# A new opening for a fused recurrence and feed-forward kernel: larger first blocks and rows, casts held back, and more inputs turned by the transposing DMA

## The chip, the cores and the metric

The kernel runs on one core of one Trainium2 chip. The metric is the device time of one execution in microseconds (us). The median of the kernel before is 418.55 us over four runs (418.23 to 419.21).

## The reference

Two stages, fused in the kernel. The first is a gated recurrence along the sequence, independent for each of 4 sequences and 256 channels; the second is a feed-forward layer with the maximum of two projections.

```python
sig = 1.0 / (1.0 + np.exp(-f_logit))                    # x, f_logit: 4 x 6144 x 256, float32
f = lower_bound + (1.0 - lower_bound) * sig             # lower_bound: 256
for t in range(S):
    h = f[:, t] * h + (1.0 - f[:, t]) * x[:, t]
    y[:, t] = h
h1, h2 = y @ w1, y @ w2                                 # w1, w2: 256 x 1024
return np.maximum(h1, h2) @ w_out                       # w_out: 1024 x 256
```

## The kernel before

The kernel walks through 24,576 tokens in blocks of 512. It runs the recurrence as scans on DVE with channels on partitions (128 x 512, 1.26 us each), so f and x have to be turned from token-major to channel-major. There are two ways to do that, chosen per chunk of 1024 tokens:

- **By PE.** GpSimd starts a DMA that casts the float32 chunk to bfloat16 in SBUF, and PE transposes it in tiles of 128 x 128.
- **By the transposing DMA.** GpSimd starts a DMA that casts the chunk into a scratch buffer in DRAM; when it has landed, SP starts a transposing DMA from there into SBUF (`fT`, `xT`). There are six scratch buffers for f and six for x.

```python
sizes = [256, 256, 512] if b == 0 else []              # first chunks of the first sequence
sizes += [CH] * ((S - sum(sizes)) // CH)               # CH = 1024
...
def by_xbar(c, s):                                     # s: 0 is f, 1 is x
    return c >= 5 and (s == 0 or c % 4 != 3)
...
NSCR = 6
scratch = [[dram.tile([CH, D], BF16, name=f"scr{s}_{q}") for q in range(NSCR)] for s in range(2)]
...
def fetch(c):
    ...
        elif by_xbar(c, s):
            scr = scratch[s][uses[s] % NSCR]
            uses[s] += 1
            nc.gpsimd.dma_start(out=scr[0:nt, :].rearrange("(p i) d -> p (i d)", p=P),
                                in_=src.rearrange("(p i) d -> p (i d)", p=P))
            held[c, s] = scr
        else:
            nat = natpool.tile([P, CH // P, D], BF16, name=("fn", "xn")[s])
            nc.gpsimd.dma_start(out=nat[:, 0 : nt // P, :],
                                in_=src.rearrange("(i p) d -> p i d", p=P))

def cross(c):
    ...
            nc.sync.dma_start_transpose(out=dst[:, :, 0:nt], in_=held[c, s][0:nt, :])
...
def gate(j):                                           # Sigmoid on ACT, from fT or from PSUM
    nc.scalar.activation(out=u[:, :, 0:nb], in_=turned[j, 0], func=AF.Sigmoid, scale=-1.0)
...
LEAD_FETCH = 10                                        # how many blocks ahead casts are written down
LEAD_CROSS = 5                                         # the same for transposing DMAs
...
for j in range(1, NBLK + 1):
    ahead("fetch", fetch, j + LEAD_FETCH)
    ahead("cross", cross, j + LEAD_CROSS)
    for fc in range(FC):                               # eight slots per block
        if j < NBLK:
            first_layer(j, fc)                         # 2 matmuls of 512 columns, Relu on ACT
        second_layer(j - 1, fc)                        # 5 matmuls of 256 columns
        ...                                            # an eighth of the PE transposes of block j + 2
        if fc < len(scans):
            scans[fc]()                                # a step of the recurrence of block j + 1, on DVE
        if fc == FC // 2 and j + 2 < NBLK:
            gate(j + 2)
```

GpSimd runs its list of casts as fast as it can. Apart from waits, mostly of about 2 us, for an earlier DMA to land, what stops it is a scratch buffer whose transpose has not been read yet. The main loop has no hold on it.

## Time and profile before

| | before |
|---|---|
| time, median | 418.55 us |
| PE busy | 395.5 of 415.8 us |
| a steady block of 512 tokens | 7.82 us, or 8.26 us with 8 PE transposes of x in it |
| main loop begins | 25.7 us |
| first transposing DMA for f: issued, landed | 33.3, 64.0 us |

The first lines are of the profile page of the kernel before: the span, PE's busy row, and three rows of 40 slices of 10.4 us each. A digit is the busy share in tenths, PEclk the granted clock in tenths.

```profile
span 415.8 us, 7247 instructions
PE 395.5 (95%) x2872; PEld 304.8 (73%) x2920; DVE 239.3 (58%) x354; ACT 274.1 (66%) x457; POOL 30.9 (7%) x57
...
PE   2699997999999999999999999999999999999996
...
PEclk9989998999999999999999999999999999999999
DMA  8998989999799999999999999872852453811212
```

PE sets the pace once it runs; what is lost is lost early, in the first two slices and in the seventh (62 to 73 us). The next lines are of the chain of waits of the kernel before (start us, duration us, what), from its early part.

```profile
2.50 6.76 DMA xn<-in_x_dram
...
9.54 23.77 DMA scr_0_90<-in_f_logit_dram
...
33.33 30.69 DMA fT<-scr_0_90
```

Up to 64 us the chain is nearly all DMA. One transposing DMA of half a megabyte takes 30.69 us, and PE then stands still for lack of it. The stretches of 5 us (busy us of each engine, granted clock, DMA share, GB/s) show how much:

```profile
55.00:60.00 5.00, 4.95 (x38) 3.72 (x35) 2.79 (x6) 2.92 (x6) 0.00 (x0) 1.00 1.01 218
60.00:65.00 5.00, 2.88 (x21) 2.14 (x20) 2.76 (x3) 0.98 (x2) 0.46 (x1) 1.00 0.86 149
65.00:70.00 5.00, 4.29 (x21) 2.59 (x21) 1.22 (x3) 3.11 (x7) 0.94 (x2) 0.66 1.10 270
```

The first number after the length is PE: 4.95, then 2.88, then 4.29 us at a clock of 0.66. The waits of 40 to 80 us (who waited for whom: us, times, longest) name both sides of it:

```profile
POOL scr_0_90 L104 <- DMA fT<-scr_0_90: 22.8, 1, 22.8
...
ACT u L160 <- DMA fT<-scr_0_90: 4.0, 1, 4.0
```

ACT wanted the data 4.0 us before they came. GpSimd (POOL) had run out of free scratch buffers 22.8 us before.

### The profile page before, as it was taken

What the parts mean: (1) busy time and instruction counts of PE and PEld (TensorE: products, weight loads), DVE (VectorE), ACT (ScalarE), POOL (GpSimd) and SP (SyncE); (2) the same over time, 40 slices, a digit from 0 to 9 for tenths busy, and PEclk for the clock granted to TensorE, in tenths of its full rate; (3) what the DMA queues carried; (4) which work ended last, traced back from release to release, by engine and by line L of the source; (5) the groups of instructions that cost most, each with busy time, mean ns of one, the idle gap of its engine ahead of it and who ended that gap; (6) DMA issues with size and microseconds to landing.
All of it is one profiled execution on the core that took longest, in us unless ns stands there. A gap on an engine that the chain in (4) does not pass through costs nothing.

```text
span 415.8 us, 7247 instructions
## 1 busy us (share of the span) xinstructions
PE 395.5 (95%) x2872; PEld 304.8 (73%) x2920; DVE 239.3 (58%) x354; ACT 274.1 (66%) x457; POOL 30.9 (7%) x57
## 2 busy tenths in 40 slices
PE   2699997999999999999999999999999999999996
PEld 2487774777777777777777777777777777777775
DVE  2545563665665764665665566566476575566641
ACT  2667655766766766776776676676676676677662
POOL 8122001000001000010010010000000000000000
PEclk9989998999999999999999999999999999999999
DMA  8998989999799999999999999872852453811212
GB/s 192 233 232 199 223 178 230 261 240 110 135 196 217 268 249 122 237 207 173 245 251 192 184 224 251 202 177 89 192 123 82 151 112 92 203 52 50 99 54 102
DMA packets 100657, 73.09 MB, mean 176 GB/s; under 512 B 79040, under 2 KB 93888, under 8 KB 100032
## 3 DMA queue, kind: packets, MB, share of 16 engines
q1 hardware_dynamic: 87152, 46.93, 49.4%
q0 software_dynamic: 13184, 25.43, 37.6%
q8 instruction: 23, 0.38, 0.3%
q10 hardware_dynamic: 288, 0.26, 0.2%
q14 instruction: 10, 0.08, 0.1%
HBM read 53.48 MB, written 44.56 MB: 236 GB/s over the span
## 4 chain that ended last, share of the span: by engine, by line
PE 83%; DMA 15%; issue 1%; ACT 0%; POOL 0%; DVE 0%; POOLq 0%; ACTq 0%
PE psO L330 48%; PE dT L301 34%; DMA fT<-scr_0_90 7%; DMA scr_0_90<-in_f_logit_dram 6%; DMA xn<-in_x_dram 2%; PE tT L151 1%; ACT u L160 0%; POOL fn L111 0%; ACT rt L309 0%; DVE osb L339 0%; POOL ident_f masks.py:199 0%; POOL ident_f masks.py:197 0%; POOLq masks.py:199 0%; ACTq L160 0%; POOLq L439 0%
## 5 line engine op out<-in xcount | busy, mean ns | idle before, releaser
L309 ACT ACTIVATE rt<-dT 128x512 bf16<-128x512 f32 (+1 forms) x392 | 225.7, 587 | 117.8 <-PE dT L301 115.7
L330 PE MATMUL psO<-wob,rt 128*128 128x256 bf16 x1536 | 230.8, 273 | 2.3
L301 PE MATMUL dT<-y,wd 128*128 128x512 bf16 (+1 forms) x736 | 221.6, 378 | 10.1 <-DVE wd L257 7.0
L330 PEld LDWEIGHTS <-rt 128*128 128x128 bf16 x1536 | 169.6, 113 | 42.9 <-issue 0.6
L350 DVE COPY osb<-psO 128x512 f32<-128x512 f32 x94 | 65.0, 692 | 153.0 <-PE psO L330 153.0
L194 DVE TENSOR_TENSOR_SCAN y<-ff,y,v 128x512 bf16<-128x512 bf16 (+1 forms) x90 | 109.2, 1255 | 0.0
L301 PEld LDWEIGHTS <-wd 128*128 128x128 bf16 x784 | 71.9, 98 | 16.9 <-DVE wd L257 9.5
L330 PE MATMUL psO<-w_122,y 128*128 128x256 bf16 x384 | 73.7, 273 | 0.3
L330 PEld LDWEIGHTS <-y 128*128 128x128 bf16 x384 | 43.3, 113 | 41.6 <-issue 0.6
L160 ACT ACTIVATE u<-fT 128x1024 bf16<-128x1024 bf16 x42 | 44.0, 1048 | 4.0 <-DMA fT<-scr_0_90 4.0
L174 DVE TENSOR_SCALAR ff<-u,nom 128x512 bf16<-128x512 bf16 (+1 forms) x98 | 29.7, 347 | 0.0
L151 PE MATMUL tT<-ident,xn 128*128 128x128 bf16 x124 | 23.6, 228 | 0.0
L184 DVE TENSOR_TENSOR v<-u,xT 128x1024 bf16<-128x1024 bf16 x32 | 21.8, 681 | 2.2 <-DMA xT<-scr_0_96 2.2
L184 DVE TENSOR_TENSOR v<-u,tT 128x1024 bf16<-128x1024 bf16 (+1 forms) x17 | 11.3, 664 | 7.6 <-PE tT L151 4.0
L151 PEld LDWEIGHTS <-xn 128*128 128x128 bf16 x124 | 12.3, 103 | 0.3
L251 ACT ACTIVATE w1s<-w1n,om 128x256 f32<-128x256 f32 x8 | 3.6, 500 | 7.1 <-DMA w1n<-in_moe_w_dram 7.1
L194 DVE TENSOR_TENSOR_SCAN y<-ff,v 128x512 bf16<-128x512 bf16 (+1 forms) x8 | 8.3, 1074 | 0.0
L111 POOL DMA_DIRECT2D xn<-in_x_dram x9 | 7.9, 883 | 2.3 <-DMA xn<-in_x_dram 2.2
L160 ACT ACTIVATE u<-tT 128x1024 bf16<-128x1024 bf16 (+2 forms) x7 | 6.3, 898 | 2.1 <-PE tT L151 2.1
L257 DVE SCALAR_TENSOR_TENSOR wd<-w2n,om,w1s 128x256 bf16<-128x256 f32 x8 | 3.5, 479 | 4.5 <-ACT w1s L251 4.5
L151 PE MATMUL tT<-ident,fn 128*128 128x128 bf16 x44 | 6.1, 245 | 0.0
L104 POOL DMA_DIRECT2D scr_0_90<-in_f_logit_dram x4 | 2.0, 500 | 49.5 <-DMA fT<-scr_0_90 49.0
(40 smaller groups left out, 49.0 us busy)
## 6 DMA issues: line engine op xcount, KB each, us to landing
out_dram<-osb SPq DMA_DIRECT2D x46, 512.0 KB, 3.8
xn<-in_x_dram POOLq DMA_DIRECT2D x7, 512.0 KB, 15.0
scr_0_90<-in_f_logit_dram POOLq DMA_DIRECT2D x4, 512.0 KB, 9.0
scr_1_91<-in_f_logit_dram POOLq DMA_DIRECT2D x4, 512.0 KB, 7.3
scr_2_92<-in_f_logit_dram POOLq DMA_DIRECT2D x4, 512.0 KB, 14.1
scr_0_96<-in_x_dram POOLq DMA_DIRECT2D x3, 512.0 KB, 19.9
scr_1_97<-in_x_dram POOLq DMA_DIRECT2D x3, 512.0 KB, 9.9
scr_3_93<-in_f_logit_dram POOLq DMA_DIRECT2D x3, 512.0 KB, 8.6
```

The source lines that it names most:

```text
L111: nc.gpsimd.dma_start(out=nat[:, 0 : nt // P, :], in_=src.rearrange("(i p) d -> p i d", p=P),)
L151: nc.tensor.transpose(dst, src, ident[:] if src.dtype == BF16 else ident_f[:])
L160: nc.scalar.activation(out=u[:, :, 0:nb], in_=turned[j, 0], func=AF.Sigmoid, scale=-1.0)
L174: nc.vector.tensor_scalar(out=ff[:, h, 0:nb], in0=u[:, h, 0:nb], scalar1=nom[:, h : h + 1], scalar2=1.0, op0=ALU.mult, op1=ALU.add,)
L184: nc.vector.tensor_tensor(out=v[:, :, 0:nb], in0=u[:, :, 0:nb], in1=turned[j, 1], op=ALU.mult)
L194: nc.vector.tensor_tensor_scan(out=y[:, h, 0:nb], data0=ff[:, h, 0:nb], data1=v[:, h, 0:nb], initial=init, op0=ALU.mult, op1=ALU.add,)
L251: nc.scalar.mul(w1s[:, kc, gcols(g)], w1n[:, kc, gcols(g)], om[:, kc : kc + 1])
L257: nc.vector.scalar_tensor_tensor(out=wd[:, kc, gcols(g)], in0=w2n[:, kc, gcols(g)], scalar=om[:, kc : kc + 1], in1=w1s[:, kc, gcols(g)], o ...
L301: nc.tensor.matmul(dT[:, 0:nb], lhsT=wd[:, kc, fc * P : (fc + 1) * P], rhs=y[:, kc, 0:nb], start=(kc == 0), stop=(kc == KC - 1),)
L309: nc.scalar.activation(out=rt[:, 0:nb], in_=dT[:, 0:nb], func=AF.Relu)
L330: nc.tensor.matmul(ps[:, r, :], lhsT=left, rhs=right, start=(s == 0 and (r == 0 or j == NBLK - 1)), stop=(s == n - 1 and (r == 1 or j == N ...
L350: nc.vector.tensor_copy(out=osb[:, 2 * g : 2 * g + 2, :], in_=ps[:])
```

## The change

Its intent is to start the main loop earlier and take work off PE. The first chunks get 512 tokens, the weights come in halves with rows of 2 KB instead of quarters with rows of 1 KB, and f and x of the first chunk in rows of 4 KB. Casts wait until the weights are nearly in, by two copies of a single column (128 x 1) on GpSimd that read the weights' tiles. In exchange f is turned by DMA from the fifth chunk on (index 4), and x from the sixth on without exception. Cut to its core:

```diff
-        sizes = [256, 256, 512] if b == 0 else []
+        sizes = [TB] * 4 if b == 0 else []
@@
     def by_xbar(c, s):
-        return c >= 5 and (s == 0 or c % 4 != 3)
+        return c >= (4, 5)[s]
@@ fetch, first chunk: a plain load in 4 KB rows, then a cast on DVE
-                    out=nat[:], in_=src.rearrange("(i p) d -> p i d", p=P)
-                )
+                    out=raw[:], in_=src.rearrange("(p i) d -> p i d", p=P)
+                )
+                nat = natpool.tile([P, CH // P, D], BF16, name=("fn", "xn")[s])
+                nc.vector.tensor_copy(out=nat[:, 0 : nt // P, :], in_=raw[:])
@@ fetch, other chunks for PE: four neighbouring tokens in one row
-                    in_=src.rearrange("(i p) d -> p i d", p=P),
+                    in_=src.rearrange("(k p i) d -> p k (i d)", p=P, i=TB // P),
@@ weights
-    NG = 4
+    NG = 2
+    def pool_waits(t):
+        nc.gpsimd.tensor_copy(out=waited[:], in_=t)
@@
-    LEAD_CROSS = 5
+    LEAD_CROSS = 3
@@ opening
+        pool_waits(w1n[0][:, 0, 0:1])
+        nc.gpsimd.dma_start(out=wob[:]..., in_=moe_w_out...)
+        pool_waits(w2n[1][:, 0, 0:1])
+        ...                                        # first layer of block 0 here
+        fetch(1)
+        fetch(2)
+        ...
-        for j in range(1, NBLK + 1):
+        for j in range(2, NBLK + 1):
@@ loop: the Sigmoid of a block turned by DMA now stands in slot 0 of the block before it
+            if j + 1 < NBLK and by_xbar(blocks[j + 1][3], 0):
+                gates[0] = j + 1
```

(Left out: the PE transposes write, and ACT and DVE read, in an order that suits the new rows; the opening runs blocks 0 and 1 outside the loop.)

More of the change, by code (lines that the diff above doesn't have):

```diff
@@ L95, in fetch @@
             if c == 0:
-                nat = const.tile([P, nt // P, D], FP32, name=("f0", "x0")[s])
+                raw = const.tile([P, nt // P, D], FP32, name=("f0", "x0")[s])
                 nc.sync.dma_start(
-                    out=nat[:], in_=src.rearrange("(i p) d -> p i d", p=P)
+                    out=raw[:], in_=src.rearrange("(p i) d -> p i d", p=P)
                 )
+                nat = natpool.tile([P, CH // P, D], BF16, name=("fn", "xn")[s])
+                nc.vector.tensor_copy(out=nat[:, 0 : nt // P, :], in_=raw[:])
                 held[c, s] = nat
@@ L111, in fetch @@
                 nc.gpsimd.dma_start(
-                    out=nat[:, 0 : nt // P, :],
-                    in_=src.rearrange("(i p) d -> p i d", p=P),
+                    out=nat[:, 0 : nt // P, :].rearrange(
+                        "p (k i) d -> p k (i d)", i=TB // P
+                    ),
+                    in_=src.rearrange(
+                        "(k p i) d -> p k (i d)", p=P, i=TB // P
+                    ),
                 )
@@ L133, in turn_steps @@
                 continue
-            if c == 0:
-                dst = ps_t.tile([P, KC, nb], FP32, name="tT")
-            else:
-                dst = ps_t.tile([P, KC, TB], BF16, name="tT")
-            turned[j, s] = dst[:, :, 0:nb]
-            for q in range(nb // P):
+            dst = ps_t.tile([P, KC, TB], BF16, name="tT")
+            ns = nb // P
+            turned[j, s] = dst[:, :, 0:nb].rearrange("p k (i m) -> p k m i", i=ns)
+            for q in range(ns):
                 for h in range(KC):
@@ L150, in turn @@
         for dst, src in steps:
-            nc.tensor.transpose(dst, src, ident[:] if src.dtype == BF16 else ident_f[:])
+            nc.tensor.transpose(dst, src, ident[:])
     ys = {}
@@ L159, in gate, with like @@
         u = midpool.tile([P, KC, TB], BF16, name="u")
+        src = turned[j, 0]
         nc.scalar.activation(
-            out=u[:, :, 0:nb], in_=turned[j, 0], func=AF.Sigmoid, scale=-1.0
+            out=like(u[:, :, 0:nb], src), in_=src, func=AF.Sigmoid, scale=-1.0
         )
         us[j] = u
+    def like(t, src):
+        if len(src.shape) == 3:
+            return t
+        return t.rearrange("p k (m i) -> p k m i", m=P)
     def scan_steps(j):
@@ L183, in drive @@
         def drive():
+            src = turned[j, 1]
             nc.vector.tensor_tensor(
-                out=v[:, :, 0:nb], in0=u[:, :, 0:nb], in1=turned[j, 1], op=ALU.mult
+                out=like(v[:, :, 0:nb], src),
+                in0=like(u[:, :, 0:nb], src),
+                in1=src,
+                op=ALU.mult,
             )
@@ L218 @@
     ident = const.tile([P, P], BF16)
-    nc.vector.tensor_copy(out=ident[:], in_=ident_f[:])
     om = const.tile([P, KC], FP32)
@@ L222 @@
     lbc = const.tile([P, KC], FP32)
+    waited = const.tile([P, 1], FP32)
     warm = const.tile([P, 1], FP32)
-    nc.sync.dma_start(out=lbc[:], in_=lower_bound.rearrange("(h p) -> p h", p=P))
-    nc.vector.tensor_scalar(
-        out=om[:], in0=lbc[:], scalar1=-1.0, scalar2=1.0, op0=ALU.mult, op1=ALU.add
-    )
-    nc.vector.tensor_scalar_add(out=nom[:], in0=lbc[:], scalar1=-1.0)
-    w1n = wpool.tile([P, KC, DFF], FP32)
-    w2n = wpool.tile([P, KC, DFF], FP32)
     wob = wpool.tile([P, FC, D], BF16)
@@ L236, with half, fcs @@
     w13 = wpool.tile([P, KC, D], BF16)
-    NG = 4
-    def gcols(g):
-        return slice(g * DFF // NG, (g + 1) * DFF // NG)
+    NG = 2
+    NQ = FC // NG
+    w1n = [wpool.tile([P, KC, NQ * P], FP32, name=f"w1n{g}") for g in range(NG)]
+    w2n = [wpool.tile([P, KC, NQ * P], FP32, name=f"w2n{g}") for g in range(NG)]
+    def half(w, g):
+        return w[g][:].rearrange("p kc (m q) -> p kc q m", q=NQ)
+    def fcs(w, kc, g):
+        return w[:, kc, g * NQ * P : (g + 1) * NQ * P].rearrange(
+            "p (q m) -> p q m", q=NQ
+        )
     def fetch_w(g):
+        cols = slice(g * DFF // NG, (g + 1) * DFF // NG)
         for w, src in ((w2n, moe_w2), (w1n, moe_w1)):
             nc.sync.dma_start(
-                out=w[:, :, gcols(g)],
-                in_=src[:, gcols(g)].rearrange("(kc p) f -> p kc f", p=P),
+                out=w[g][:],
+                in_=src[:, cols].rearrange("(kc p) f -> p kc f", p=P),
             )
@@ L250, in make_w1s @@
         for kc in range(KC):
-            nc.scalar.mul(
-                w1s[:, kc, gcols(g)], w1n[:, kc, gcols(g)], om[:, kc : kc + 1]
-            )
+            nc.scalar.mul(fcs(w1s, kc, g), half(w1n, g)[:, kc], om[:, kc : kc + 1])
+    def pool_waits(t):
+        nc.gpsimd.tensor_copy(out=waited[:], in_=t)
     def make_wd(g):
@@ L257, in make_wd @@
             nc.vector.scalar_tensor_tensor(
-                out=wd[:, kc, gcols(g)],
-                in0=w2n[:, kc, gcols(g)],
+                out=fcs(wd, kc, g),
+                in0=half(w2n, g)[:, kc],
                 scalar=om[:, kc : kc + 1],
-                in1=w1s[:, kc, gcols(g)],
+                in1=fcs(w1s, kc, g),
                 op0=ALU.mult,
@@ L264, in make_wd, with make_w1T @@
             )
-    def make_w1T(g):
-        n = FC // NG
-        pt = ps_o.tile([P, KC, n, P], FP32, name="psO")
+    def make_w1T(k):
+        pt = ps_o.tile([P, KC, 2, P], FP32, name="psO")
         for kc in range(KC):
-            for q in range(n):
-                fc = n * g + q
+            for q in range(2):
+                fc = 2 * k + q
                 nc.tensor.transpose(
@@ L274, in make_w1T @@
                 )
-        dst = w1T[:, n * g : n * g + n, :].rearrange("p q (k d) -> p k q d", k=KC)
-        if g % 2:
-            nc.scalar.copy(out=dst, in_=pt[:])
-        else:
-            nc.vector.tensor_copy(out=dst, in_=pt[:])
+        dst = w1T[:, 2 * k : 2 * k + 2, :].rearrange("p q (k d) -> p k q d", k=KC)
+        nc.scalar.copy(out=dst, in_=pt[:])
     def make_w13():
@@ L367 @@
     with tc.manual_schedule():
+        nc.sync.dma_start(out=lbc[:], in_=lower_bound.rearrange("(h p) -> p h", p=P))
+        nc.vector.tensor_copy(out=ident[:], in_=ident_f[:])
+        nc.vector.tensor_scalar(
+            out=om[:], in0=lbc[:], scalar1=-1.0, scalar2=1.0, op0=ALU.mult, op1=ALU.add
+        )
+        nc.vector.tensor_scalar_add(out=nom[:], in0=lbc[:], scalar1=-1.0)
         fetch(0)
-        fetch(1)
         for g in range(NG):
             fetch_w(g)
-        nc.gpsimd.dma_start(
-            out=wob[:], in_=moe_w_out.rearrange("(fc p) c -> p fc c", p=P)
-        )
-        fetch(2)
         nc.scalar.activation(out=warm[:], in_=om[:, 0:1], func=AF.Sigmoid)
@@ L383 @@
         make_w1s(1)
-        make_wd(0)
-        first_layer(0, 0)
-        first_layer(0, 1)
-        turn(turn_steps(1))
-        make_wd(1)
-        recurrence(1)
-        first_layer(0, 2)
-        first_layer(0, 3)
-        make_w1s(2)
-        make_wd(2)
+        pool_waits(w1n[0][:, 0, 0:1])
+        nc.gpsimd.dma_start(
+            out=wob[:].rearrange("p (g q) c -> p g (q c)", g=NG),
+            in_=moe_w_out.rearrange("(g p q) c -> p g (q c)", g=NG, q=NQ),
+        )
+        pool_waits(w2n[1][:, 0, 0:1])
+        make_wd(0)
+        for fc in range(0, NQ):
+            first_layer(0, fc)
+        fetch(1)
+        fetch(2)
+        done["fetch"] = 3
+        ahead("fetch", fetch, LEAD_FETCH)
+        make_wd(1)
         make_w1T(0)
         make_w1T(1)
-        first_layer(0, 4)
-        first_layer(0, 5)
-        make_w1s(3)
-        make_wd(3)
+        for fc in range(NQ, FC):
+            first_layer(0, fc)
         make_w1T(2)
-        first_layer(0, 6)
-        first_layer(0, 7)
         make_w1T(3)
-        turn(turn_steps(2))
-        gate(2)
-        make_w13()
-        done["fetch"] = 3
-        ahead("fetch", fetch, LEAD_FETCH)
-        ahead("cross", cross, LEAD_CROSS)
-        for j in range(1, NBLK + 1):
+        make_w13()
+        turn(turn_steps(1))
+        recurrence(1)
+        for fc in range(FC):
+            second_layer(0, fc)
+        turn(turn_steps(2))
+        recurrence(2)
+        for fc in range(FC):
+            first_layer(1, fc)
+        turn(turn_steps(3))
+        gate(3)
+        for j in range(2, NBLK + 1):
             ahead("fetch", fetch, j + LEAD_FETCH)
@@ L413 @@
             steps = turn_steps(j + 2) if j + 2 < NBLK else []
-            scans = scan_steps(j + 1) if j + 1 < NBLK else []
+            gates = {}
+            if j + 1 < NBLK and by_xbar(blocks[j + 1][3], 0):
+                gates[0] = j + 1
+            if j + 2 < NBLK and not by_xbar(blocks[j + 2][3], 0):
+                gates[FC // 2] = j + 2
+            scans = []
             for fc in range(FC):
@@ L420 @@
                 turn(steps[fc * n // FC : (fc + 1) * n // FC])
+                if fc in gates:
+                    gate(gates[fc])
+                if fc == 0 and j + 1 < NBLK:
+                    scans = scan_steps(j + 1)
                 if fc < len(scans):
                     scans[fc]()
-                if fc == FC // 2 and j + 2 < NBLK:
-                    gate(j + 2)
 _INS = ['x', 'f_logit', 'lower_bound', 'moe_w1', 'moe_w2', 'moe_w_out']
```

## The prediction

> **What bounds it now.** The busy table has the tensor engine (PE) at 395.5 of 415.8 us. In the timeline its stream is gapless: a slot is two 512-column matmuls (0.43 us) and five 256-column ones (0.53), a 512-token block takes 7.8 us, a PE transpose adds 0.055. The losses are early: the main loop starts at 25.7 us, PE is busy only 2.88 us of the stretch 60 to 65, and the clock halves for 3.4 us near 21 and 65 us, costing about 1.7 us each time.
>
> The chain of waits is DMA until 64.1 us: casts, then one transposing DMA (first f chunk, issued 33.3, landed 64.0). The transfer records show why: casts into DRAM move as 32 KB packets of 2.43 us, transposes as 256-byte packets of 0.018. Between 50 and 60 us each DMA engine passed about two small packets per large one, so the transpose, 128 small packets per engine, hardly moved until GpSimd ran out of scratch slots (last cast issued 41.3, drained near 61). [...]
>
> **What the change does.**
> 1. PE transposes fall from 48 f and 128 x to 32 and 48: 96 x 0.055 = 5.3 us, 4.4 of it inside the saturated loop.
> 2. Opening: 3 MiB of f, x and weights in 2 and 4 KB rows (84 and 159 ns a packet) without casts beside them land near 11 us instead of 19. Two 128x1024 casts on DVE (about 1 us each) and 512-token scans (2.45) move the first matmul from 11 to about 14 us, but eight full slots follow. The loop at j=2 starts near 31 us; against equal work 4 to 5 us earlier than before.
> 3. But casts start near 10 us, and block 4 needs the first transposed f at about 40 us, where before block 7 needed it at 61. Only the six scratch slots stop the casts of chunks 4 to 9. Chunk 4 starts near 20 us; twelve casts of 2.45 us and two outputs drain near 52; the transpose lands near 54 to 56. So I expect a PE stall of 12 to 16 us between 41 and 56 us, in block 3.
> 4. Afterwards cast, transposes and output of a chunk take about 12.5 us of DMA in 15.6 of PE: no lasting stall.
>
> **Sum.** PE resumes at 56.5; left are half a block (3.9), 44 blocks of 7.82 (344), half clock (1.7), chunk 4's x (0.5) and the end (4.7): 354.8. Span 411, time (2.5 above span) **413.5 us, range 403 to 419**. Chances: faster by over 2% 0.28, within 2% 0.67, slower 0.05.
>
> **What would show it.** Right: weights landed by 12 us; in the chain of waits the first fT DMA lasting 25 us or more, landing at 52 to 58, with the Sigmoid waiting 10 us or more for it; low PE slices at 41 to 56; 7.8 us a block throughout; 80 transposes. Wrong: fT landing before 45, or new waits for fT or xT later, since transposes are issued three blocks ahead instead of five.
>
> **What would make it wrong.** If transposes get more turns between casts, no stall: about 400 us. If casts start later or run slower, the stall grows one for one: 417 or more. A second stall at chunk 5 would add up to 3 us.

The resumption at 56.5 us and the 354.8 us after it make the span of 411.3 us.

## The result and the profile after

| | before | after | predicted |
|---|---|---|---|
| time, median | 418.55 us | 419.52 us (418.53 to 419.99) | 413.5, range 403 to 419 |
| last part of w1 reaches ACT | 19.4 us | 13.3 us | landed near 11 |
| first matmul of the first layer | 11.1 us | 13.1 us | 14 |
| first fT landed | 64.0 us | 58.6 us | 54 to 56 |
| PE's stall for it | 2.8 us | 12.8 us | 12 to 16 |
| PE resumes | 65.7 us | 60.3 us | 56.5 |
| steady blocks | 7.82 and 8.26 us | 7.82 us | 7.82 |

The ratio is 1.0018, 95% interval 0.9994 to 1.0042: the same. A ratio here is the mean time of one kernel's fast runs over that of the kernel before in the same rounds, so it is not quite the ratio of the medians quoted. The span of the profiled run was 418.2 us, its time 419.99.

The page of the kernel after, the same rows:

```profile
span 418.2 us, 6999 instructions
PE 388.8 (93%) x2761; PEld 296.7 (71%) x2808; DVE 246.5 (59%) x345; ACT 273.3 (65%) x446; POOL 27.9 (7%) x59
...
PE   2799529999999999999999999999999999999996
...
PEclk9999859999999999999999999999999999999999
DMA  7899998999969969979969979989745743744212
```

PE has 6.7 us less to do, yet the span is longer: the hole has moved to the fifth and sixth slices and grown. The chain of waits of the kernel after:

```profile
2.69 7.96 DMA w1n_118<-in_moe_w_dram
10.71 1.23 POOL waited L269
...
16.13 11.30 DMA scr_0_90<-in_f_logit_dram
...
31.45 27.16 DMA fT<-scr_0_90
58.72 1.06 ACT u L165
```

The casts' wait on GpSimd now heads the chain, and one transposing DMA of 27.16 us ends it. The stretches of 5 us:

```profile
45.00:50.00 5.00, 2.43 (x20) 1.89 (x19) 0.00 (x0) 0.00 (x0) 0.00 (x0) 1.00 1.06 228
50.00:55.00 5.00, 0.00 (x0) 0.00 (x0) 0.00 (x0) 0.00 (x0) 0.00 (x0) 0.51 0.76 163
55.00:60.00 5.00, 0.00 (x0) 0.00 (x0) 0.19 (x1) 1.28 (x2) 0.86 (x2) 0.50 1.16 236
60.00:65.00 5.00, 4.69 (x23) 2.81 (x23) 4.52 (x6) 2.68 (x6) 0.10 (x1) 0.62 1.38 274
```

From 47.5 to 58.7 us no engine computes, while the DMA engines go on working. The waits of 40 to 70 us:

```profile
POOL scr_0_90 L106 <- DMA fT<-scr_0_90: 22.3, 1, 22.3
...
ACT u L165 <- DMA fT<-scr_0_90: 14.3, 1, 14.3
...
PE dT L313 <- ACT rt L321: 12.8, 1, 12.8
```

Read from below: PE waits 12.8 us for a PSUM tile that a Relu on ACT has to free; ACT has the Sigmoid in front of that Relu in its list and stands at it for 14.3 us; the Sigmoid waits for the transposing DMA. GpSimd is out of scratch buffers 22.3 us before that DMA lands, as before. The trace's own transfer records show what the DMA engines do meanwhile. This is a count of packets begun in a stretch (us from the start of the span, as everywhere here), on all 16 engines. The transposing DMA moves in packets of 256 bytes, the output of the main loop in packets of 4 KB; both are in SP's queue, and the first output stands in front of the first transposing DMA there:

```
kernel    stretch us     casts into scratch           SP's queue: 256 B   SP's queue: 4 KB
before    50 to 60       64 of 32 KB, 2.43 us each    129                 0
after     35.5 to 46.5   63 of 32 KB                  0                   128
after     46.6 to 54     48 of 32 KB                  82                  0
after     54 to 58.2     2 of 32 KB                   1966                30
```

A cast of 1024 tokens is 16 packets of 32 KB (those of the first one begin within 0.55 us and last 2.43 us each, so one per engine); a transposing DMA is 2048 small packets, by estimate 128 for each of the 16 engines. Beside casts an engine here passed about two packets of SP's queue between one 32 KB packet and the next, 2.43 us later, whether these two were of 4 KB (128 to 63) or of 256 bytes (129 to 64, 82 to 48). When the casts had run dry, all the rest went through within 5 us.

### The profile page after: what moved, and what is told of

Same layout as the page of the kernel before. It is cut to its first block, busy times and chain, and to the rows that moved or that the text cites. A ratio compares the mean times of both kernels' runs of the same rounds, so it can differ in the third digit from the quotient of the medians.

```text
span 418.2 us, 6999 instructions
## 1 busy us (share of the span) xinstructions
PE 388.8 (93%) x2761; PEld 296.7 (71%) x2808; DVE 246.5 (59%) x345; ACT 273.3 (65%) x446; POOL 27.9 (7%) x59
## 4 chain that ended last, share of the span: by engine, by line
PE 84%; DMA 12%; POOL 1%; issue 1%; SPq 0%; ACT 0%; DVE 0%; ACTq 0%
PE psO L342 49%; PE dT L313 35%; DMA fT<-scr_0_90 6%; DMA scr_0_90<-in_f_logit_dram 3%; DMA w1n_118<-in_moe_w_dram 2%; DMA scr_4_94<-in_f_logit_dram 1%; POOL fn L113 0%; POOL xn L113 0%; POOL waited L269 0%; ACT u L165 0%; SPq L97 0%; ACT rt L321 0%; SPq L380 0%; SPq L259 0%; DVE osb L351 0%
## 5 line engine op out<-in xcount | busy, mean ns | idle before, releaser
L321 ACT ACTIVATE rt<-dT 128x512 bf16<-128x512 f32 x384 | 222.8, 598 | 109.2 <-PE dT L313 109.1
L313 PE MATMUL dT<-y,wd 128*128 128x512 bf16 x721 | 219.8, 383 | 18.7 <-ACT rt L321 12.8
L208 DVE TENSOR_TENSOR_SCAN y<-ff,y,v 128x512 bf16<-128x512 bf16 x88 | 107.8, 1266 | 0.0
L195 DVE TENSOR_TENSOR v<-u,xT 128x1024 bf16<-128x1024 bf16 x42 | 29.1, 692 | 57.8 <-ACT u L165 57.8
L165 ACT ACTIVATE u<-fT 128x1024 bf16<-128x1024 bf16 x44 | 46.2, 1050 | 14.3 <-DMA fT<-scr_0_90 14.3
L184 DVE TENSOR_SCALAR ff<-u,nom 128x512 bf16<-128x512 bf16 x96 | 29.2, 346 | 0.0
L195 DVE TENSOR_TENSOR v<-u,tT 128x1024 bf16<-128x1024 bf16 x6 | 7.3, 1221 | 28.0 <-ACT u L165 26.8
L208 DVE TENSOR_TENSOR_SCAN y<-ff,v 128x512 bf16<-128x512 bf16 x8 | 9.3, 1206 | 0.0
L165 ACT ACTIVATE u<-tT 128x1024 bf16<-128x1024 bf16 x4 | 4.2, 1050 | 7.7 <-PE tT L155 7.6
L155 PE MATMUL tT<-ident,xn 128*128 128x128 bf16 x48 | 6.5, 236 | 0.2 <-DVE xn L101 0.2
L106 POOL DMA_DIRECT2D scr_0_90<-in_f_logit_dram x4 | 2.0, 505 | 49.3 <-DMA fT<-scr_0_90 49.3
L106 POOL DMA_DIRECT2D scr_3_93<-in_f_logit_dram x4 | 1.9, 486 | 38.3 <-DMA fT<-scr_3_93 37.5
L106 POOL DMA_DIRECT2D scr_2_92<-in_f_logit_dram x4 | 1.9, 486 | 37.5 <-DMA fT<-scr_2_92 36.8
```

Of the source, the lines that this page charges most:

```text
L155: nc.tensor.transpose(dst, src, ident[:])
L165: nc.scalar.activation(out=like(u[:, :, 0:nb], src), in_=src, func=AF.Sigmoid, scale=-1.0)
L184: nc.vector.tensor_scalar(out=ff[:, h, 0:nb], in0=u[:, h, 0:nb], scalar1=nom[:, h : h + 1], scalar2=1.0, op0=ALU.mult, op1=ALU.add,)
L195: nc.vector.tensor_tensor(out=like(v[:, :, 0:nb], src), in0=like(u[:, :, 0:nb], src), in1=src, op=ALU.mult,)
L208: nc.vector.tensor_tensor_scan(out=y[:, h, 0:nb], data0=ff[:, h, 0:nb], data1=v[:, h, 0:nb], initial=init, op0=ALU.mult, op1=ALU.add,)
L313: nc.tensor.matmul(dT[:, 0:nb], lhsT=wd[:, kc, fc * P : (fc + 1) * P], rhs=y[:, kc, 0:nb], start=(kc == 0), stop=(kc == KC - 1),)
```

## The experiments

The theory is **starvation**: the first transposing DMA lands only when the casts in front of it run dry, so the number of casts in front decides when PE can go on. Rival 1: the transposing DMA is slow of itself, or issued too late (31.5 us, behind the first output in SP's queue). Rival 2: fewer casts in front are paid for later. Rival 3: it is bytes on the DMA engines that count, not packets.

Each kernel below ran four times, in three groups of rounds on three chips. The kernel before ran seven times in each group: medians 419.3, 420.2 and 419.8 us, single runs 417.9 to 422.6. The ratios are against those runs.

### Fewer buffers, first try: a wrong result

```diff
-    NSCR = 6
+    NSCR = 3          # slots3;  4 in slots4
```

> The changed kernel with three scratch buffers per input instead of six, so GpSimd can have only six casts of the later chunks in front of the first transposing DMA instead of twelve. Theory (starvation: casts in 32 KB packets keep the 256-byte transposing packets from their turns until the casts run dry): each buffer less takes two casts, 4.9 us, away from the landing of the first fT (58.6 us); it lands near 44 us, where the Sigmoid asks for it at 44.4; the 12.8 us PE stall and the half clock after it (1.9 us) vanish; 405 us, ratio about 0.965. Rival 1 (the transpose itself is late or slow, because it is issued at 31.5 us behind the first output and takes 27 us by itself): landing and time unchanged, 418 to 420. Rival 2 (prefetch depth is needed later): the first stall goes but new waits for fT or xT appear later and the gain is lost.

> Four scratch buffers per input: the dose in between. Theory: the first fT lands near 48.8 us, PE stalls from 47.4 to about 50.5, some half clock after it; about 409 to 410 us, ratio 0.977. Rivals as for three buffers.

Both gave a wrong result (relative errors 1.02 and 0.11), at 419.6 and 414.3 us. The edit was faulty: casts were still written down ten blocks ahead, so that the cast of a later chunk into a buffer stood in the program before the transpose that should read the earlier one. In the program's order the transpose would thus read the later chunk; the same edit with a shorter lead gives right results (next section). Their times answer another question and are left aside.

### Fewer buffers, in the right order

```diff
-    NSCR = 6
+    NSCR = 3          # three_slots;  4 in four_slots;  2 in two_slots
-    LEAD_FETCH = 10
+    LEAD_FETCH = 7    # 9 in four_slots;  5 in two_slots
```

> The changed kernel with three scratch buffers per input instead of six, and the program's lead for casts cut from ten blocks to seven, so that no cast is written down ahead of the transpose that reads its buffer (the fault of the earlier try). Six casts now stand in front of the first transposing DMA, not twelve. Starvation theory: it lands near 43 to 44 us instead of 58.6, about when the Sigmoid asks for it (44.4); the 12.8 us PE stall and the 1.9 us of half clock go; about 405 us, ratio 0.965, and the result is right. Rival 1 (the transpose is slow of itself or issued late): landing and time unchanged. Rival 2 (a shallow prefetch is paid later): new waits for fT or xT after 60 us, time over 410.

> Four scratch buffers per input, lead for casts nine blocks: the dose in between, eight casts in front. Starvation theory: two casts, 4.9 us, later than with three: first fT lands near 48 to 49 us, PE stalls about 3 us from 47.4 on; about 409 us, ratio 0.976. Rivals as for three.

> Two scratch buffers per input, lead for casts five blocks: four casts in front of the first transpose. Theory: fT lands near 39 us, 5 us before it is asked for, so the last 2.2 us of the Sigmoid's wait (0.7 us of PE) go: 404 to 404.5 us, and no new wait for fT or xT, since a buffer is refilled some 25 us before it is read. Rival: with two buffers the casts come too late and transposes wait for them; over 408 us.

| buffers per input | casts up to the stop | first fT issued, landed (us) | ACT waits for it | PE stall | time, median | ratio (95%) |
|---|---|---|---|---|---|---|
| 6 (the change) | 12 | 31.5, 58.6 | 14.3 | 12.8 | 419.52 | 1.0018 (0.9994 to 1.0042) |
| 4 | 8 | 30.8, 48.7 | 5.1 | 3.6 | 409.10 | 0.9732 (0.9689 to 0.9774) |
| 3 | 6 | 30.5, 45.6 | 2.2 | 0.7 | 405.11 | 0.9638 (0.9588 to 0.9688) |
| 2 | 4 | 30.5, 38.5 | none | none | 404.40 | 0.9645 (0.9595 to 0.9695) |

Results are right in all three. The casts are counted from chunk 4 on. One of them, of x of chunk 4, goes to SBUF in 2 KB packets, so the casts in 32 KB packets are 11, 7, 5 and 3. The lead had to change along with the number of buffers, and was not varied alone; but in all these traces what GpSimd's list stops at is a cast that waits for the transpose of fT to free its buffer, and that depends on the number of buffers. The Sigmoid in question and the PE matmul after it, from the timeline (start us, duration us, engine, what, in brackets the idle time before it), with four buffers:

```profile
48.82 1.06 ACT L165 ACTIVATE u<-fT 128x1024 bf16<-128x1024 bf16 x1 [5.06 <-DMA fT<-scr]
50.41 0.59 PE L313 MATMUL dT<-y,wd 128*128 128x512 bf16 x2 [3.59 <-ACT rt L321]
```

and with three:

```profile
45.66 1.06 ACT L165 ACTIVATE u<-fT 128x1024 bf16<-128x1024 bf16 x1 [2.19 <-DMA fT<-scr]
47.26 0.59 PE L313 MATMUL dT<-y,wd 128*128 128x512 bf16 x2 [0.72 <-ACT rt L321]
```

From twelve casts to four the landing moves by 20.1 us, 2.5 us per cast, with steps of 9.9, 3.1 and 7.1 us where 9.8, 4.9 and 4.9 were expected. The issue hardly moves. So rival 1 falls: a transposing DMA issued at the same 30.5 us lands after 8.0 us when little is in front of it. Rival 2 falls too: the page of the kernel with two buffers has no second hole, and a PE that is busy 97% of the span.

```profile
span 402.6 us, 7054 instructions
PE 388.5 (97%) x2808; PEld 295.3 (73%) x2808; DVE 246.6 (61%) x345; ACT 273.3 (68%) x446; POOL 27.5 (7%) x59
...
PE   3699999999999999999999999999999999999996
```

With two buffers the kernel beats both given kernels by about 3.5%. Between two and three buffers nothing is decided: 404.40 against 405.11 us, on different chips.

### The same cure for the kernel before

```diff
-    NSCR = 6
+    NSCR = 2
-    LEAD_FETCH = 10
+    LEAD_FETCH = 6
```

> The kernel before with two scratch buffers per input instead of six, lead for casts six blocks instead of ten. Starvation theory: its own stall (first fT landed 64.0, PE idle about 3 us near 62 to 65, 1.7 us lost to half clock after it) goes, since only four of the eleven casts in 32 KB packets are left in front; fT lands before 50 us; about 413.5 us, ratio 0.988. Rival (the kernel before was not held up by its casts): 418 as before.

Measured: 414.10 us (411.17 to 414.72), ratio 0.9839 (0.9784 to 0.9894), verdict unclear at 2%, result right. Its first fT, issued at 33.9 us, landed 11.4 us later, ACT never waited for fT, and the clock stayed full after 26 us. The kernel before was held by the same thing, for about a third of what the change made of it.

### Without the hold

```diff
-        pool_waits(w1n[0][:, 0, 0:1])
-        pool_waits(w2n[1][:, 0, 0:1])
```

> The changed kernel without the two waits that hold the casts back. If the DMA engines simply have a fixed amount of work before the first transpose gets through, only the idle gap of the DMA near 10 to 13 us is saved: first fT lands near 55 us, first PE matmul of the first layer moves from 13 to 18 us or later, but PE still has to wait for fT; about 416 us. If the stall follows the start of the casts one for one, as the prediction put it, casts start 11 us earlier, fT lands near 48 us and the time is about 408 us.

Measured: 418.46 us, ratio 0.9956 (0.9912 to 0.9999). Neither account had it quite. Casts of tokens are now issued from 2.5 us on instead of 13.0, and the last 32 KB packets begin near 50 us instead of 54: casts started 10.5 us earlier end about 4 us earlier. The first fT lands at 57.1 us, as its issue, behind the first output, has moved to 44.9 us; and PE does not wait for fT at all, because the loop is late itself. The chain of waits of this kernel:

```profile
3.84 22.31 DMA w1n<-in_moe_w_dram
26.17 2.29 ACT w1s L266 x2
```

The last half of w1, which now shares the DMA engines with the casts, takes 22.31 us to come and lands at 26.2 us instead of 13.3. The main loop begins near 48 us. The hold had brought the weights 13 us earlier, and PE then spent these 13 us waiting for f instead.

### Three buffers, without the hold

> Three scratch buffers and no hold of the casts: fills the fourth cell of the table (hold or not, six buffers or three). Without the hold the weights share the DMA engines with the early casts and the last of them landed at 26.2 us instead of 13.3, so that the loop began near 48 us and PE was never short of fT; fewer buffers cannot help there. Theory (the hold is worth a lot once the stall is gone, and nothing before): 417 to 419 us, 12 us or more above the 405.1 of three buffers with the hold. Rival (hold and buffers act independently; the hold was worth minus 1 us with six buffers): about 404 us.

Measured: 418.02 us, ratio 0.9968 (0.9926 to 1.0010). That is as the theory had it, and 14 us from the rival. The four cells together (medians, us):

| | six buffers | three buffers |
|---|---|---|
| casts held back | 419.52 | 405.11 |
| casts not held back | 418.46 | 418.02 |

The cells are from different groups of rounds, which matters little at this size. Each of the two measures alone is worth nothing. Together they are worth 13 us: one lets the weights through first, the other lets the first transposes through next.

### x of every fourth chunk on PE again

Three buffers and the hold, and of the change only this undone:

```diff
-        return c >= (4, 5)[s]
+        return c >= (4, 5)[s] and (s == 0 or c % 4 != 3)
```

> Three buffers, but x of the chunks 7, 11, 15, 19 and 23 turned by PE again, as in the kernel before. This prices the part of the change that moves x to the transposing DMA, in a kernel without the stall. Theory: 80 PE transposes of 0.055 us come back into a saturated PE: plus 4.4 us, 409.5 us; blocks of 8.26 us beside those of 7.82. Rival (moving x to the DMA gains nothing, because its load is paid in waits elsewhere): 405 us.

Measured: 409.29 us, ratio 0.9755 (0.9714 to 0.9795), by medians 4.2 us above three buffers (in another group of rounds; by the ratios 4.9). The PE transposes of x went from 48 to 128, and without them there had been no wait for xT either: the part that moves x to the DMA is worth what PE had spent on it.

### Smaller packets for the casts

In `rows2k` the casts into scratch write 2 KB per packet and in `rows512` 512 bytes; order, bytes and the six buffers stay.

```diff
-    out=scr[0:nt, :].rearrange("(p i) d -> p (i d)", p=P),
-    in_=src.rearrange("(p i) d -> p (i d)", p=P),
+    out=scr[0:nt, :].rearrange("(k p i) d -> p k (i d)", p=P, i=TB // P),   # rows2k
+    in_=src.rearrange("(k p i) d -> p k (i d)", p=P, i=TB // P),
+    # rows512: "(i p) d -> p i d" on both sides
```

> The changed kernel, six buffers, but the scratch casts walk rows so that each packet writes 2 KB instead of 32 KB: the same bytes, the same order, the same number of casts in front. Theory (turns by packet): each DMA engine meets 16 packets per cast instead of one, so the 128 transposing packets per engine get their turns within four to eight casts; the first fT lands at 44 to 55 us instead of 58.6; 405 to 415 us. Rival 3 (the casts' bytes take the DMA engines' time, whatever the packets): lands at 58 or later, since a cast in 2 KB packets is a little slower (0.173 us per 2 KB against 2.43 us per 32 KB, so 2.8 against 2.4 us).

> The changed kernel with six buffers, but scratch casts in rows of 512 bytes: same bytes, same order, twelve casts in front. With rows of 2 KB the DMA engines passed one transposing packet per cast packet (466 to 434 in 5 us), so the 128 packets per engine still took until the casts ran dry. With 512-byte packets of 0.059 us, turns by packet let them through in about 128 x 0.1 us after the issue at 31 us and the first output: fT lands at 44 to 48 us instead of 58.6, PE stalls 3 us or less at first, although the casts as a whole are slower (3.8 us each) and may bring later waits: 405 to 416 us. Rival 3 (the bytes ahead in order decide): fT lands at 60 us or later, 421 us or more.

`rows2k`: 421.46 us, ratio 1.0043 (1.0001 to 1.0084); fT landed at 59.6 us. As a time this is what rival 3 expected, and the theory's number was wrong. The packets show why:

```
kernel    stretch us   casts into scratch     SP's queue: under 512 B
rows2k    45 to 50     444 of 2 KB            474
rows512   40 to 45     1067 of 512 B          1081
```

The engines now pass one small packet per cast packet, not two. In 45 to 50 us the transpose has moved by 474 packets, where with large packets it moved by 82 in 46.6 to 54 us, but 128 turns of 0.18 us (5 us on 16 engines, 444 turns) are by estimate still 23 us, as long as the casts last. `rows512` makes a turn short enough (1067 in 5 us: 0.075 us): its first fT, issued at 31.4 us, landed 15.0 us later at 46.4, with all twelve casts in the same order, in the window that the theory gave and 12 us before six buffers with large packets. By then the casts had moved only 5.6 of the eleven half megabytes for the scratch buffers; with 32 KB packets all eleven had gone when the first fT landed. So it is not the bytes in front that decide, which is against rival 3. The reservation: this profile is of a run in the slow state (430.5 us span). Its four runs were 418.59, 429.06, 432.27 and 434.79 us, so no time is compared, and only the early landing is read from it. As a time the expectation (405 to 416 us) failed even for the one fast run.

### The first transpose issued earlier

```diff
+        ahead("cross", cross, 4)
         for fc in range(FC):
             second_layer(0, fc)
```

> The changed kernel with the first transposing DMA put ahead of the first output in the queue of SP, so that it is issued near 27.5 us instead of 31.5. Theory (starved until the casts are dry): it lands within 1 us of 58.6 and the time stays, 418 to 420 us. Rival 1 (late issue behind the output): it lands about 4 us earlier and the time falls by as much, to 415 us.

Issued at 26.0 us instead of 31.5, the first fT landed at about 55.7 us instead of 58.6. Three of four runs were slow (433.80 to 447.03 us, the profiled one too) and one fast at 417.56. As a time it is inconclusive. The landing moved by 2.9 us for an issue 5.4 us earlier: less than rival 1 had it, more than the 1 us that I allowed. In the slow profile ACT waits 15 times for fT, 47.3 us in all, and DVE 16 times for xT, 72.4 us; why this kernel and `rows512` fall into that state, and the others do not, was not tried and stays open.

## Why the prediction was wrong

- **Step 3, the mechanism, was right.** The first fT took 27.2 us and landed while PE stood still, and the Sigmoid waited 14.3 us. That PE's wait of 12.8 us lay in the predicted 12 to 16 is partly luck, for both of its ends came late: the loop at j = 2 began at 34.8 us, not near 31, so that the Sigmoid asked at 44.4 us, not at about 40; and the data landed at 58.6 us, not at 54 to 56. Taking casts away from in front of it removed the stall in three doses, 419.5 to 404.4 us. The counts of packets above agree with two queues that take turns, 82 small beside 48 of 32 KB, and 1081 beside 1067 when both are small.
- **Step 3, its size, was wrong:** "PE resumes at 56.5" measured 60.3 us, 3.8 us late. The term that failed is the start of chunk 4: its first 32 KB packet began at 24.1 us, not "near 20", and the last cast ended at 56.4 us, not "near 52"; the 32 us between them were as predicted. I let the casts "start near 10 us" from the time of single packets (84 and 159 ns, sixteen engines). But the opening's loads moved 315 GB/s in the stretch 5 to 10 us, not the 390 to 412 that those packets give. The first half of w1 was in at 10.7 us, the one-column copy on GpSimd that marks it took 1.23 us more, and the first casts of tokens were issued at 13.0 us. That is 3.0 of the 4.1 us; the rest is not broken down.
- **The sum, its last term, was wrong:** "the end (4.7)" measured 8.0 us, from 410.2, where the second layer of the last block stands alone, to 418.2. I had found it as a remainder from the kernel before, after misplacing that kernel's stall: I counted half a block as still to do (3.3 us), but the timeline shows PE resuming with the first slot of the next one. Terms with a trace behind them should be read there and not be left as a remainder.
- Put together: 411.3 + 3.8 + 3.1 (357.9 us from the resumption to the end, against 354.8) is 418.2 us, the span measured. The time lay 1.8 us above the span instead of 2.5.
- **Step 1 was right:** 80 transposes, blocks of 7.82 us throughout, and 4.2 us for the x part where it could pay.
- **Step 2, the gain of the opening, was of the right size, but only where it can be seen.** Three buffers with x on PE (409.3) against the kernel before with two (414.1) leaves 4.8 us by medians, or 3.5 us by ratios (0.0084 of 419). It is an estimate across two groups of rounds, and the two kernels differ a little beside the opening too (f of one chunk more goes by DMA). The traces say the same: the block that starts at token 2048 begins its Relus at 55.5 us in the kernel before (56.7 with two buffers), and at 51.2 in the changed kernel with two buffers, 4.3 to 5.5 us earlier. The step's two casts on DVE took 0.69 us each, not about 1.
- **Step 4 was right:** no second wait for fT or xT. After the stall every block took 7.82 us. The 12.5 us of DMA per chunk were an estimate; from the packets of the kernel before (2.43 us for a cast, 0.018 and 0.159 us for packets of 256 bytes and 4 KB, 16 engines) it comes to about 12.0.
- **One sentence was wrong in kind:** "If casts start later or run slower, the stall grows one for one". Casts that start 10.5 us earlier end 4 us earlier and delay the weights by 13 us. With the hold, the busy share of the DMA engines was 0.58 from 10 to 15 us and 0.87 to 1.44 in the stretches from 15 to 50 us; without it, 0.98 to 1.38 from 5 to 50 us. (The share counts the packets' durations, so it can exceed 1.) There was little left to fill but the gap that the hold makes: the order of the transfers could change, their sum hardly.

Where the expected gain went, by medians: the change gains about 4.8 us in the opening and 4.2 us by x, and loses 10 us more to the first fT than the kernel before did. That last figure is the difference between 419.5 - 405.1 = 14.4 us, what three buffers recover from the change, and 418.5 - 414.1 = 4.4 us, what two buffers recover from the kernel before. These are differences between groups of rounds, and the three figures add up by construction; by ratios they are 3.5, 4.9 and 9.2 us. The clock is a part of the 14.4: PE idle for 12.8 us, then 3.5 us at half clock. The records show half clock from 50.1 to 63.8 us: the clock halved when PE had stood for 2.6 us, and was full again when PE had worked for 3.5 us. The last point of the list below has more.

## What to carry to other kernels

Here a prefetch that could run as deep as its buffers allowed was a queue in front of what the same DMA engines had to deliver next, 2.5 us per cast; count what stands in front of the first transfer that somebody will wait for, and let the number of buffers bound it. When two queues share the engines, compare the sizes of their packets: 256 bytes against 32 KB meant two small packets in 2.43 us here. And a measure that brings something forward shows its worth only when the next thing in line is there too, so test such measures in pairs before dropping one.

## What else the traces show

- The casts from DRAM to DRAM moved in packets of 32 KB, 2.43 us each (median, kernel before). In the kernel after, the first transposing DMA beside them took 27.2 us from issue to landing, where an undisturbed one took 4.7 us (the first one with three buffers and no hold).
- A product on DVE of bf16 with one operand in PSUM took 677 ns for 128 x 1024 (median), against 681 ns with both in SBUF. In the kernel after, where the operand in PSUM is read in steps of 4 elements, it took 1221 ns, against 691 ns with both in SBUF.
- Two gaps of PE and the clock: 2.8 us of idle PE came with half clock for 3.413 us in the kernel before, and 3.6 us with four buffers did not (granted clock 1.00 throughout). In the traces before and after, the changes of clock lie whole multiples of 3.413 us apart. So the length of the gap alone does not decide whether the clock halves; what does was not shown.
